# Retention attention into a cosine-gated FFN on one core: a re-planned order, separate scores, and other engines for casts and decay

## The chip, the cores and the metric

The kernel runs on one NeuronCore of a Trainium2 chip. Five engines work from their own instruction queues: TensorE (PE, matrix products; PEld is its weight load), VectorE (DVE), ScalarE (ACT), GpSimd (POOL) and SyncE (SP). DMA transfers are issued from the queues of SP, POOL and ACT and are carried out by 16 DMA engines. The metric is the device time of one execution in microseconds (us). The median of seven runs of the kernel before is 211.03 us (209.88 to 214.27).

## What is computed

Inputs q, k and v are (4 batches, 8 heads, 768 positions, 64), with a decay `lam` per head. Attention is linear with a causal mask and decay, computed over blocks of 64 positions with a carried state:

```python
for b in range(nb):
    intra = np.einsum('bhic,bhjc->bhij', qb, kb) * Dmask[None]
    intra = np.einsum('bhij,bhjd->bhid', intra, vb)
    inter = np.einsum('bhid,bhde->bhie', qb * lam_pow[None], kv_state)
    out[:, :, sl] = intra + inter
    kv_state = lam_block[None, :, None, None] * kv_state + np.einsum('bhsd,bhse->bhde', kb * rev_pow[None], vb)
```

Its output, as 3072 tokens of 512 features, is x of an FFN: `h = x @ w_in` (512 to 2048), `g = h * cos(h)`, `out = g @ w_out` (2048 to 512). All inputs are float32; the kernel multiplies in bfloat16.

## The kernel before

The 3072 tokens are 24 blocks of 128 tokens. Since a decay from position j to i is lam to the power i − j, the kernel multiplies q by one exponential of the position and another operand by the inverse exponential; the mask is then plain 0 and 1 and states need no factor between blocks.

**Opening: two spans.** The first 256 positions of batches 0 and 1 (`SPANS = 2`, blocks 0 to 3) are done by `add_span` in a layout of their own. Six loads (`add_span_load`) of 512 KB each, q0 k0 q1 k1 v0 v1, go out on SP. In `prep` (L547) q is multiplied by `q_sp` and v by `v_sp` into bfloat16, in halves of four heads; who does it stands in `QV` (q by DVE, v by POOL). `prep_k` (L551) casts k on ACT. PE transposes q and k (L558), `transposes_out` (L561) copies them out of PSUM, `scores` (L569) multiplies, `scores_out` (L574) applies the mask on DVE, `values` (L596) and `carried` (L602) make the attention output, `update` (L583) the state for the second half of a span, and `values_out` (L610) casts the output to `xT`, the FFN's input. Meanwhile PE runs idle matmuls (`keep_awake`, L803) in the gaps that the plan foresees.

**Weights.** `add_w` loads w_in in five chunks (`W_IN`, in units of 128 hidden columns: 3, 3, 4, 3, 3) and w_out in four, cast to bfloat16 by the DMA itself, from POOL's queue (L263). The first chunk waits until k1 has landed.

**Pairs.** The remaining 20 blocks are ten pairs, 2 to 11; a pair is the same positions of two batches. `prepare` loads q, k, v (six 256 KB loads on SP, L263), multiplies q and v by the exponentials and casts k, mostly on POOL (L326, L330, L334), and transposes q and k: pair 2 on PE (L356), pairs 3 to 11 by two DMA transposes from SP's queue (L362). `add_scores` makes scores (L404), masks them (L409) and updates the running state (`update` L416, `state` L422), whose bfloat16 copy `S` `state_16` makes on POOL (L427). `add_stretch` makes the values (L465), the part carried by the state (L493) and casts the result to `xT` (L501). Normally the scores and update of the next pair are interleaved in a stretch, between the values of one half and the other; a pair listed in `ALONE` has its scores by themselves, ahead of its own stretch, and the stretch before it begins its second part with a drain of PE.

**FFN.** Blocks are grouped in tiles of four or two (`TILES = [4, 2, 2, 2, 2, 4, 4, 4]`). For each tile and each of 16 groups of 128 hidden columns `hidden` (L683) makes h with four matmuls, `cosine` (L689) runs on ACT, `gated` (L695) on DVE. For the first tile the first `SPLIT` = 4 groups come in two halves, so that the blocks of the first span can start alone. `project` (L726) makes the output of a block, `project_out` (L740) copies it, `store_out` (L747, L749) stores it from SP's queue. PE alternates between hidden products of a tile and output products of the tile before.

**The order.** No queue's order is written by hand. Every instruction is a task with an engine, a duration in us, dependencies and a priority; `Planner.order` runs a list schedule over these estimates and emits the instructions in the order that results. DMAs are two tasks: an issue on a queue and a transfer on one engine called DMA, with a latency `lat` after it. Loads on a queue keep their listed order; transposes and stores are put in among them by the plan. The estimates shape the order alone: on the chip each engine works through its queue in that order and waits for semaphores.

Of the kernel before, what the change touches and what calls it, by code (L numbers as in the profile page):

```python
# [10 lines left out]
F32 = mybir.dt.float32  # L11
# [8 lines left out]
DMA_FROM = 6  # L20
TILES = [4, 2, 2, 2, 2, 4, 4, 4]
SPLIT = 4
BANKS = 8
LAG = 2
ATT = 0.95
ALONE = [3, 4]

QV = [[("DVE", "POOL"), ("DVE", "POOL")], [("DVE", "POOL"), ("DVE", "POOL")]]
OUTS = [{"qT": ("DVE", "DVE"), "kT": ("ACT", "ACT")}, {"qT": ("ACT", "ACT"), "kT": ("ACT", "ACT")}]
V_PRIO = {"POOL": -1.7, "DVE": 0.0}  # L30
LATE = 30.0
ORDER = "q0 k0 q1 k1 v0 v1 i0 i1 i2 i3 i4 o0 o1 o2 o3"

W_IN = [3, 3, 4, 3, 3]

# [15 lines left out]
class Planner:  # L51
# [3 lines left out]

    SETUP = {"POOL": 5.6, "DVE": 5.6, "ACT": 7.3, "SP": 1.3}

# [8 lines left out]
    def order(self):  # L66
# [5 lines left out]
        while todo:  # L72
            first = {}
            for t in todo:
                if only.get(t.eng, t) is not t:
                    continue
                at = self.ready(t, got)
                if at is None:
                    continue
                if t.banks:  # L80
                    b = self.free_banks(t, owner)
                    if len(b) < t.banks:
                        continue
                    t.bank = b[:t.banks]
                    at = max([at] + [x for x, _ in t.bank])
                at = max(at, free.get(t.eng, 0.0))
                first.setdefault(t.eng, []).append((at, t))
            best = None
            for eng, c in first.items():
                t0 = min(a for a, _ in c)  # L90
                a, t = min(((a, t) for a, t in c if a <= t0 + 1e-6), key=lambda x: x[1].prio)
                if best is None or a < best[0]:
                    best = (a, t)
            assert best, "no task can start"
            a, t = best
            t.start, t.end = a, a + t.dur
            free[t.eng] = t.end
            only.pop(t.eng, None)
            if t.then:
                only[t.eng] = t.then  # L100
            if t.get:
                got[t.get].append(t)
            if t.banks:
                t.bank = [i for _, i in t.bank]
                for j, i in enumerate(t.bank):
                    owner[i] = (t, j)
            todo.remove(t)
            done.append(t)
# [30 lines left out]
def kernel(  # L139
# [59 lines left out]
    for i in range(2):  # L199
# [18 lines left out]
                         lnl.unsqueeze(1).to_broadcast([P, NB, H]))  # L218
    v_sp = consts.tile([P, H, 2], F32)
    nc.scalar.activation(v_sp, expo_sp, AF.Exp, scale=-1.0)  # L220
    q_scale = consts.tile([P, NB, H], F32)
# [47 lines left out]
    def add_span_load(name, src, x, prio, deps):  # L269
        def emit(_):  # L270
            if ("raw", x) not in live:
                live["raw", x] = work.tile([P, 3, H, 2, D], F32, tag="g", name="sp_f")
            t = live[name, "sp", x] = live["raw", x][:, "qkv".index(name[0])]
            return start(nc.sync, t.rearrange("u h s d -> u h (s d)"),
                         src[x, :, 0:2 * P, :].rearrange("h (u s) d -> u h (s d)", s=2), deps)

        issue, load_t[name, "sp", x] = dma("SP", 1.5, 0.5, emit, prio, deps)
        return load_t[name, "sp", x]

    def add_load(n, name, src, prio, deps=()):  # L280
# [6 lines left out]

        issue_t[name, n], load_t[name, n] = dma("SP", 1.1, 0.5, emit, prio, deps, get=name)
        return load_t[name, n]
# [3 lines left out]
    def add_w(which, c, prio, deps=()):  # L293
# [7 lines left out]
        part = W_IN[c] / 4 if which == "in" else 1.0  # L301
        _, w_t[which, c] = dma("POOL", 2.6 * part, 0.8, emit, prio - 2000 if which == "in" and c < 2 else prio, deps, lat=2.8 if which == "in" and c < 2 else 1.6)
        return w_t[which, c]
# [8 lines left out]
    def prepare(pr):  # L312
# [51 lines left out]
        for i, src in enumerate((a, k_)):  # L364
            get = None if i else "qkT"
            if 2 * pr >= DMA_FROM:
                head, T[pr, i] = dma("SP", 1.2, 1.3, partial(transposes_dma, i=i), 2 * pr + i - LAG + 1.5,
                                     src + ([qkT_head[pr]] if i else []), get=get, ordered=False)
                T[pr, i].lat = 3.0
                if i and 2 * pr + LAG < NBLK:  # L370
# [20 lines left out]
    def add_scores(pr, part):  # L391
# [34 lines left out]
        def state_16(_, half):  # L426
            nc.gpsimd.tensor_copy(new_S(pr, half), live["sum", pr, half])  # L427

# [17 lines left out]
        if not last:  # L446
            y = pl.add("DVE", 0.69, [x], partial(state, half=1), pa(0.57))
            u.bank_frees.append([y])
            for half, t in enumerate((x, y)):
                if (pr, half) not in Uo:  # L450
                    Uo[pr, half] = pl.add("POOL", 0.61, [t], partial(state_16, half=half), pa(0.56 + 0.02 * half))
        qk_head[pr].frees = [T[pr, 0], T[pr, 1], u]
# [78 lines left out]

    spans, span_deps = [], []

    def add_span(x):
        pa = lambda part: -1000.0 + 2 * x + part
        pv = lambda part: -990.0 + 2 * x + part
        cut = [slice(4 * hp, 4 * hp + 4) for hp in range(2)]
        us = {"DVE": 0.69, "POOL": 1.1}
        vec = {"DVE": nc.vector, "POOL": nc.gpsimd}
        L = {name: consts.tile([P, 2, H, D], BF16, name=f"{name}_sp{x}") for name in ("q", "k", "v")}  # L540
        L.update({name: consts.tile([P, 2, NP, P], BF16, name=f"{name}_sp{x}") for name in ("qT", "kT")})
# [4 lines left out]
        def prep(_, name, hp, e):  # L546
            vec[e].tensor_mul(place(L[name], hp), live[name + "_f", "sp", x][:, cut[hp]],  # L547
                              (q_sp if name == "q" else v_sp)[:, cut[hp]].unsqueeze(3).to_broadcast([P, 4, 2, D]))

        def prep_k(_, hp):  # L550
            nc.scalar.copy(place(L["k"], hp), live["k_f", "sp", x][:, cut[hp]])  # L551

# [59 lines left out]

        so, kt, v_t = [[], []], [], []
        for hp in range(2):
            eq, ev = QV[x][hp]
            a = pl.add(eq, us[eq], [load_t["q_f", "sp", x]], partial(prep, name="q", hp=hp, e=eq), pa(-0.9 + 0.1 * hp))
            kt.append(pl.add("ACT", 0.61, [load_t["k_f", "sp", x]], partial(prep_k, hp=hp), pa(-0.9 + 0.1 * hp)))
            v_t.append(pl.add(ev, us[ev], [load_t["v_f", "sp", x]], partial(prep, name="v", hp=hp, e=ev), pa(V_PRIO[ev] + 0.1 * hp)))
            outs = []
            for name, src in (("qT", a), ("kT", kt[hp])):  # L620
                e = OUTS[x][name][hp]
                t = pl.add("PE", MM(P, 4), [src], partial(transposes, name=name, hp=hp), pa(-0.5 + 0.1 * hp), banks=1)
                outs.append(pl.add(e, 0.58 if e == "ACT" else 0.42, [t], partial(transposes_out, name=name, hp=hp, e=e), pa(-0.5 + 0.1 * hp)))
                t.bank_frees = [[outs[-1]]]
# [3 lines left out]

        u = pl.add("PE", 0.42, v_t + kt, update, -1100.0, banks=1)
        Uo_sp[x] = [pl.add(e, 0.4 if e == "ACT" else 0.42, [u], partial(update_out, h=h, e=e), -1100.0)  # L630
                    for h, e in zip(halves, ("ACT", "DVE"))]
        u.bank_frees = [Uo_sp[x]]
        span_deps.extend(v_t + kt)
        v0 = pl.add("PE", 0.35, so[0] + v_t[:1], partial(values, hp=0), pv(0.2), banks=2)
        v1 = pl.add("PE", 0.35, [v0] + so[1] + v_t[1:], partial(values, hp=1), pv(0.25))
        second = pl.add("PE", MM(P, 4) + 0.1, [v1] + Uo_sp[x], carried, pv(0.3))
        Vo[2 * x] = [pl.add("ACT", 0.6, [v1], partial(values_out, c=0, e="ACT", pairs=slice(0, NP)), pv(0.3))]
        Vo[2 * x + 1] = [pl.add(e, 0.38, [second], partial(values_out, c=1, e=e, pairs=pairs), -1200.0)
                         for e, pairs in (("ACT", slice(0, 2)), ("DVE", slice(2, 4)))]
        v0.bank_frees = [Vo[2 * x], Vo[2 * x + 1]]  # L640
# [26 lines left out]
    def add_ffn(i):  # L667
# [43 lines left out]
        for j in range(nb):  # L711
# [3 lines left out]
            for piece, part in enumerate(pieces):  # L715
# [26 lines left out]
                def store_out(_, eng, j=j, piece=piece, part=part, width=width):  # L742
                    b, c = where(n0 + j)
                    r0 = b * S + c * P
                    if n0 + j < 2 * SPANS:
                        for s, h in enumerate(halves):
# [7 lines left out]
                           get="o_sb")  # L754
                d = dma(queue, 0.7, 1.2 if n0 + j < 2 * SPANS else 0.6, partial(store_out, eng=queue), n0 + j + 8, [e], ordered=False)[1]
                e.frees = [d]
# [8 lines left out]
    for at, name in enumerate(names):  # L765
# [3 lines left out]
        if soft:  # L769
            kept.append(add_w({"i": "in", "o": "out"}[which], n, at, deps))  # L770
        elif n < SPANS and at < 15:
            kept.append(add_span_load(which + "_f", src[which], n, at - 40, deps))
        else:
# [26 lines left out]
    def keep_awake(us, at):  # L800
        cols = P if at < 5.0 else 4 * P
        for _ in range(int(us / (cols / (1200.0 if at < 5.0 else 2400.0) + 0.0025))):
            nc.tensor.matmul(idle_ps[:, :cols], lhsT=ident, rhs=blank[:, :cols], start=True, stop=True)  # L803

    now = 1.6
    for t in plan:
        if t.eng == "PE" and t.start < lead_end.start + 1e-6:
            keep_awake((t.start - now) * 0.95 if now < 2.0 else t.start - now - 0.25, now)
            now = t.end
# [32 lines left out]
```

## Time and profile before

| what | value |
|---|---|
| median of 7 runs | 211.03 us |
| profiled execution, its own time | 210.37 us |
| its span in the profile | 208.7 us |
| PE busy | 193.9 us (93%) |
| DVE, ACT, POOL busy | 111.0, 108.6, 72.2 us |
| first hidden product (L683) | 16.72 us |
| first pair load issued (SP, L263) | 33.76 us |
| last output product ends | 205.25 us |
| granted TensorE clock, mean | 0.998 |
| output products L726 / hidden products L683, busy | 89.1 / 91.2 us |
| HBM read, written | 27.27 MB, 6.29 MB |

Times are from the start of the span. A strip of the page has 40 slices of about 5.2 us, each digit a share of busy time in tenths. Rows of groups give busy time, the mean of one in ns, and the idle time before them with what ended it. In the chain and the timeline a row begins with its start and its length in us; `SPq` and `POOLq` are queues issuing DMAs. "Issue to landing" counts from the issuing instruction's start until the data is there.

### The profile page before, as it was taken

Reading aid. Unit: us, or ns where it says so; the run is one execution under the profiler, and the core shown is the slowest. Engines: PE = TensorE matmul, PEld = TensorE weight load, DVE = VectorE, ACT = ScalarE, POOL = GpSimd, SP = SyncE. Lnnn points to the kernel's source line nnn. Section 1 sums busy time; section 2 is a strip of 40 time slices with the busy share of each in tenths; the row PEclk is TensorE's granted clock in tenths of the full one; section 3 lists DMA queues with packets and bytes.
Section 4 is the critical chain, followed back from the end, with each engine's and each line's share of the span. In section 5 each row is a group of like instructions: output and inputs, shape, how many; then the busy total and the mean of one; then the engine's idle time right before and its main releaser. Section 6 shows DMA issues by size and latency. Waiting matters only on the chain.

```text
span 208.7 us, 5817 instructions
## 1 busy us (share of the span) xinstructions
PE 193.9 (93%) x2426; PEld 112.9 (54%) x2453; DVE 111.0 (53%) x209; ACT 108.6 (52%) x202; POOL 72.2 (35%) x99
## 2 busy tenths in 40 slices
PE   6869999998798999979999999999999999999993
PEld 6447444456656756856765454545444444444462
DVE  2697783263963934966754588746333333333000
ACT  5967771232907644945563676554554555355120
POOL 4099101156156384548483746570000000000000
PEclk9999999999999999999999999999999999999999
DMA  4999999999999999999999999992101110111112
GB/s 126 346 243 141 189 202 219 232 219 224 180 241 170 255 214 265 213 224 246 231 237 249 196 249 202 218 231 81 53 8 42 53 52 0 50 50 53 50 68 82
DMA packets 96234, 34.46 MB, mean 165 GB/s; under 512 B 82256, under 2 KB 93264, under 8 KB 96208
## 3 DMA queue, kind: packets, MB, share of 16 engines
q1 hardware_dynamic: 91312, 29.77, 62.3%
q0 software_dynamic: 4752, 4.19, 13.1%
q8 instruction: 19, 0.31, 0.6%
q10 hardware_dynamic: 144, 0.13, 0.2%
q14 instruction: 7, 0.06, 0.1%
HBM read 27.27 MB, written 6.29 MB: 161 GB/s over the span
## 4 chain that ended last, share of the span: by engine, by line
PE 70%; DMA 15%; SPq 5%; POOL 3%; issue 2%; ACT 2%; DVE 1%; ACTq 0%; POOLq 0%
PE ps_f L726 32%; PE ps_h L683 31%; DMA v_f<-in_v_dram 7%; DMA qkT<-qk 4%; SPq L263 4%; DMA sp_f<-in_k_dram 3%; PE ps_o L465 2%; POOL v_sp L547 1%; PE ps_kv L416 1%; DMA out_dram<-o_sb 1%; PE ps_s L404 1%; ACT cos L689 1%; PE ps_o L493 1%; POOL v_s L334 1%; POOL w_in_sb L263 1%
## 5 line engine op out<-in xcount | busy, mean ns | idle before, releaser
L695 DVE TENSOR_TENSOR g<-ps_h,cos 128x256 bf16<-128x256 f32 (+1 forms) x132 | 70.0, 545 | 54.9 <-ACT cos L689 51.9
L689 ACT ACTIVATE cos<-ps_h,halfpi 128x256 f32<-128x256 f32 (+1 forms) x132 | 71.7, 575 | 41.0 <-PE ps_h L683 40.5
L683 PE MATMUL ps_h<-xT,w_in_sb 128*128 128x256 bf16 (+1 forms) x522 | 91.2, 320 | 0.7 <-ACT o_sb L740 0.4
L726 PE MATMUL ps_f<-w_out_sb,g 128*128 128x512 bf16 (+1 forms) x381 | 89.1, 370 | 1.8 <-issue 1.3
L683 PEld LDWEIGHTS <-w_in_sb 128*128 128x128 bf16 x528 | 51.1, 98 | 34.5 <-issue 0.6
L726 PEld LDWEIGHTS <-g 128*128 128x128 bf16 x400 | 38.3, 98 | 39.0 <-issue 0.3
L326 POOL TENSOR_TENSOR qk<-q_f,q_scale 128x512 bf16<-128x512 f32 x19 | 19.4, 1044 | 33.4 <-DMA q_f<-in_q_dram 26.1
L740 ACT COPY o_sb<-ps_f 128x512 f32<-128x512 f32 (+1 forms) x24 | 13.9, 578 | 24.2 <-PE ps_f L726 21.4
L334 POOL TENSOR_TENSOR v_s<-v_f,v_scale 128x512 bf16<-128x512 f32 x19 | 19.5, 1045 | 6.4 <-DMA v_f<-in_v_dram 6.4
L501 ACT CAST xT<-ps_o 128x512 bf16<-128x512 f32 x19 | 10.2, 588 | 17.8 <-PE ps_o L493 17.0
L409 DVE TENSOR_TENSOR s_m<-ps_s,mask 128x512 bf16<-128x512 f32 x20 | 13.0, 685 | 3.3 <-PE ps_s L404 2.7
L330 POOL CAST qk<-k_f 128x512 bf16<-128x512 f32 x18 | 11.1, 614 | 8.3 <-DMA k_f<-in_k_dram 8.1
L422 DVE TENSOR_TENSOR sum<-sum,ps_kv 128x512 f32<-128x512 f32 x15 | 10.2, 682 | 0.7
L427 POOL CAST S<-sum 128x512 bf16<-128x512 f32 x15 | 9.2, 617 | 1.5 <-DVE sum L422 1.5
L465 PEld LDWEIGHTS <-v_s 64*64 64x64 bf16 x320 | 4.3, 106 | 5.1 <-issue 4.9
L404 PE MATMUL ps_s<-qkT 64*64 64x64 bf16 x320 | 4.4, 194 | 2.8 <-DMA qkT<-qk 1.6
L465 PE MATMUL ps_o<-s_m,v_s 64*64 64x64 bf16 x320 | 6.5, 197 | 0.5
L803 PE MATMUL ps_idle<-blank,ident 128*128 128x128 bf16 (+1 forms) x43 | 5.3, 314 | 1.7 <-POOL ident masks.py:199 1.6
L263 POOL DMA_DIRECT2D w_in_sb<-in_moe_w_in_dram x5 | 4.0, 802 | 6.7 <-DMA sp_f<-in_k_dram 6.7
L740 DVE COPY o_sb<-ps_f 128x256 f32<-128x256 f32 x1 | 0.4, 425 | 10.8 <-PE ps_f L726 10.8
L803 PEld LDWEIGHTS <-ident 128*128 128x128 bf16 x45 | 4.6, 141 | 1.7 <-POOL ident masks.py:199 1.6
L330 ACT CAST qk<-k_f 128x512 bf16<-128x512 f32 x2 | 1.2, 618 | 8.3 <-DMA k_f<-in_k_dram 8.3
(69 smaller groups left out, 81.3 us busy)
## 6 DMA issues: line engine op xcount, KB each, us to landing
q_f<-in_q_dram SPq DMA_DIRECT2D x20, 256.0 KB, 3.5
k_f<-in_k_dram SPq DMA_DIRECT2D x20, 256.0 KB, 4.5
v_f<-in_v_dram SPq DMA_DIRECT2D x20, 256.0 KB, 4.9
out_dram<-o_sb SPq DMA_DIRECT2D x19, 256.0 KB, 2.0
w_out_sb<-in_moe_w_out_dram POOLq DMA_DIRECT2D x4, 512.0 KB, 13.0
w_in_sb<-in_moe_w_in_dram POOLq DMA_DIRECT2D x4, 384.0 KB, 6.6
out_dram<-o_sb SPq DMA_DIRECT2D x9, 128.0 KB, 2.4
sp_f<-in_q_dram SPq DMA_DIRECT2D x2, 512.0 KB, 5.3
```

Of the source, the lines that this page charges most:

```text
L263: i = queue.dma_start(out=o, in_=x)
L326: vec[e].tensor_mul(new_qk()[:, 0, :, s], live.pop(("q_f", 2 * pr + s)), q_scale[:, c, :].unsqueeze(2).to_broadcast([P, H, D]))
L330: (nc.scalar.copy if early else nc.gpsimd.tensor_copy)(new_qk()[:, 1, :, s], live.pop(("k_f", 2 * pr + s)))
L334: vec[e].tensor_mul(live["v_s", 2 * pr + s], live.pop(("v_f", 2 * pr + s)), v_scale[:, c, :].unsqueeze(2).to_broadcast([P, H, D]))
L409: nc.vector.tensor_mul(t, live["s", pr][s], mask.unsqueeze(1).to_broadcast([P, H, D]))
L422: nc.vector.tensor_add(new, live["sum", pr, 0] if half else live["sum", pr - 1, 1], live["kv", pr][half])
L465: yield lambda h=h: nc.tensor.matmul(o[halves[h % 2], h // 2, m], lhsT=live["v_s", n0 + s][m, h, :], rhs=live["s_m", n0 + s][m, h, :], sta ...
L683: nc.tensor.matmul(t[:, :n], lhsT=w_in_sb[:, kd, f * P:(f + 1) * P], rhs=live["xT", i][:, kd, at], start=(kd == 0), stop=(kd == KD - 1))
L689: nc.scalar.activation(c[:, :n], live["h", i, f, at.start][:, :n], AF.Sin, bias=halfpi)
L695: nc.vector.tensor_mul(live["g", i][:, f, at], live.pop(("h", i, f, at.start))[:, :n], live.pop(("c", i, f, at.start))[:, :n])
L726: nc.tensor.matmul(live["f", i, j, piece][:, :width], lhsT=live["g", i][:, f, j * P:(j + 1) * P], rhs=w_out_sb[:, f, part], start=(f == 0) ...
L740: (nc.scalar.copy if eng == "ACT" else nc.vector.tensor_copy)(o[:, :width], live["f", i, j, piece][:, :width])
```

## The change

Four things change together, and with them the plan and so the order of every queue.

1. **Estimates.** Loads are planned with 1.22 us of transfer and 0.85 of issue, stores, DMA transposes, weights and span loads with other durations and latencies; the DMA engine of the plan is free only from 2.9 us, and its tasks are served in the order of their issue. `keep_awake` fills the planned gaps without the margin of 0.25 us.
2. **Structure.** `ALONE` holds pairs 3 to 6 instead of 3 and 4. The tile of pairs 6 and 7 is split into two tiles of one pair. `SPLIT` is 3. w_in comes in four chunks (3, 5, 4, 4).
3. **State casts.** The 15 casts in `state_16` of `add_scores` move from POOL to ACT. (The one of `add_span_state` stays on POOL.)
4. **Spans.** The inverse exponential multiplies k instead of v: in span 0 by DVE, in span 1 by POOL. v of span 0 is cast to bfloat16 by its DMA, which moves to POOL's queue and waits for k0's landing; v of span 1 stays on SP, waits for k1's landing, and is cast by POOL and ACT in halves. The first weight chunk no longer waits for k1; the second is planned after span 1's k multiplies, the fourth after its v casts. All transposed q and k are copied out by ACT. The second span's output casts are split between ACT and DVE, the first span's are on ACT.

```diff
-TILES = [4, 2, 2, 2, 2, 4, 4, 4]
-SPLIT = 4
+TILES = [4, 2, 2, 2, 2, 2, 2, 4, 4]
+SPLIT = 3
-ALONE = [3, 4]
-QV = [[("DVE", "POOL"), ("DVE", "POOL")], [("DVE", "POOL"), ("DVE", "POOL")]]
-OUTS = [{"qT": ("DVE", "DVE"), "kT": ("ACT", "ACT")}, {"qT": ("ACT", "ACT"), "kT": ("ACT", "ACT")}]
+LOAD_US = 1.22
+ALONE = [3, 4, 5, 6]
+QK = [{"q": ("DVE", "DVE"), "k": ("DVE", "DVE")}, {"q": ("DVE", "DVE"), "k": ("POOL", "POOL")}]
+OUTS = [{"qT": ("ACT", "ACT"), "kT": ("ACT", "ACT")}, {"qT": ("ACT", "ACT"), "kT": ("ACT", "ACT")}]
+VALUES_OUT = [[("ACT",), ("ACT",)], [("ACT", "DVE"), ("ACT", "DVE")]]
-ORDER = "q0 k0 q1 k1 v0 v1 i0 i1 i2 i3 i4 o0 o1 o2 o3"
+ORDER = "q0 k0 q1 k1 v0 v1 i0 i1 i2 i3 o0 o1 o2 o3"
-W_IN = [3, 3, 4, 3, 3]
+W_IN = [3, 5, 4, 4]
...
-        issue_t[name, n], load_t[name, n] = dma("SP", 1.1, 0.5, emit, prio, deps, get=name)
+        issue_t[name, n], load_t[name, n] = dma("SP", LOAD_US, 0.85, emit, prio, deps, get=name, lat=1.0)
...
-                head, T[pr, i] = dma("SP", 1.2, 1.3, partial(transposes_dma, i=i), 2 * pr + i - LAG + 1.5,
+                head, T[pr, i] = dma("SP", 1.4, 1.3, partial(transposes_dma, i=i), 2 * pr + i - LAG + 1.5,
-                T[pr, i].lat = 3.0
+                T[pr, i].lat = 1.2
...
         def state_16(_, half):
-            nc.gpsimd.tensor_copy(new_S(pr, half), live["sum", pr, half])
+            nc.scalar.copy(new_S(pr, half), live["sum", pr, half])
...
-        def prep_k(_, hp):
-            nc.scalar.copy(place(L["k"], hp), live["k_f", "sp", x][:, cut[hp]])
+        def cast_v(_, hp):
+            (nc.scalar.copy if hp else nc.gpsimd.tensor_copy)(span_v[x][:, cut[hp]], live["v_f", "sp", x][:, cut[hp]])
...
+            v_t = [[pl.add(("POOL", "ACT")[hp], 0.61, [load_t["v_f", "sp", x]], partial(cast_v, hp=hp), pa(-1.0 + 0.1 * hp))] for hp in range(2)]
+            w_t["in", 3].issue.deps += v_t[0] + v_t[1]
+            late = w_t["in", 1].issue
...
-                d = dma(queue, 0.7, 1.2 if n0 + j < 2 * SPANS else 0.6, partial(store_out, eng=queue), n0 + j + 8, [e], ordered=False)[1]
+                d = dma(queue, 1.2 if n0 + j < 2 * SPANS else 0.9, 1.7 if n0 + j < 2 * SPANS else 0.75, partial(store_out, eng=queue), n0 + j + 8, [e], ordered=False)[1]
...
-            keep_awake((t.start - now) * 0.95 if now < 2.0 else t.start - now - 0.25, now)
+            keep_awake((t.start - now) * 0.95 if now < 2.0 else t.start - now, now)
```

## The prediction

> **What bounds the kernel now.** I read five views, from wide to narrow. The page's first part says who is busy, its strip says whether transfers are:
>
> ```profile
> PE 193.9 (93%) x2426; PEld 112.9 (54%) x2453; DVE 111.0 (53%) x209; ACT 108.6 (52%) x202; POOL 72.2 (35%) x99
> ...
> DMA  4999999999999999999999999992101110111112
> ```
>
> TensorE is idle for 208.7 − 193.9 = 14.8 us. The DMA engines are at nine tenths or more from 5 to about 140 us, so until there the arrival of data can set what TensorE waits for; after it nothing loads. Next the waits of PE:
>
> ```profile
> PE ps_s L404 <- DMA qkT<-qk: 1.6, 2, 1.4
> ...
> PE ps_o L596 <- POOL v_sp L547: 1.3, 2, 0.8
> PE ps_s L404 <- DVE g L695: 1.0, 1, 1.0
> ...
> PE ps_o L493 <- POOL S L427: 0.4, 1, 0.4
> PE ps_h L683 <- ACT o_sb L740: 0.4, 1, 0.4
> ```
>
> The columns are total, times, longest. The first wait is for transposed q and k that come by DMA. The second belongs to the opening, the others to the middle. I placed each with the timeline. Then the chain that ended last, for the opening:
>
> ```profile
> 4.11 5.99 DMA sp_f<-in_k_dram
> 10.09 0.30 issue
> 10.39 1.25 POOL w_in_sb L263 x2
> 11.65 0.50 issue
> 12.15 3.06 POOL v_sp L547 x3
> 15.24 0.42 PE ps_o L596 x16
> ```
>
> The reader sees k of the second span land at 10.10, two weight issues that waited for it on GpSimd, and the four v multiplies behind those. The timeline has the last multiply end at 16.20, and the hidden product run unbroken from 17.87, with one of its 0.435 us groups done before. Its equivalent start is 17.87 − 0.435 = 17.43. Last, SyncE's own waits and the same chain in the middle:
>
> ```profile
> SPq L362 <- POOL S L427: 8.7, 5, 2.4
> SPq L362 <- POOL v_s L334: 8.1, 9, 1.3
> ...
> 48.06 0.59 ACT xT L501
> 48.72 2.51 DMA out_dram<-o_sb
> 51.33 0.59 ACT o_sb L740
> 51.97 2.38 PE ps_h L683 x20
> ...
> 85.99 4.89 DMA qkT<-qk
> 90.93 0.45 PE ps_s L404 x32
> ```
>
> SyncE's queue stands still behind GpSimd's casts; ACT stands still for 2.69 us (48.64 to 51.33) for a store to free an output buffer; and pair 6's scores start 1.35 us after PE was ready.
>
> From 92 us on, PE does FFN blocks and stretches with hardly an idle piece. So three places can change: the opening, the middle (45 to 92 us), and the instructions PE executes.
>
> **The opening.** Removed are four GpSimd v multiplies of 1.04 us (4.05 us in the timeline) and four ACT casts of k (0.617). Added are k multiplies, two on VectorE (0.69) and two on GpSimd (1.04), and casts of v only for the second span (about 0.61 each, one on GpSimd and one on ACT; row L330). The other v is cast by its own DMA from GpSimd's queue, with no compute.
>
> ACT gains two transposed-q copies (0.59 instead of VectorE's 0.42). ACT is free of its table load only at 7.43, and its copies of the first span then end near 9.8, about when scores began before (9.69). VectorE has q and k of the first span, then q of the second: from 5.63 to about 9.9, against masks that began at 10.22. Both are hidden.
>
> Three moves decide. First, **v of span 0** waits on GpSimd for k of span 0 (about 6.9: both k loads average 5.6 us to landing, the later took 5.99), is issued by 7.9, and at the 6.1 us median of v lands near 14.0. Then come 0.42 values, 0.40 carried, 0.6 copy: first hidden product near 15.5, not 16.72. Second, **v of span 1** moves behind a new wait on SyncE for k of span 1: 10.1 + 6.1 = 16.2, cast 0.61, values 0.42, carried 0.40, copy 0.4: 18.1, against a last copy that ends at 18.74. Behind it on SyncE stand only pair loads, due after 30 us. The k path is not later: 10.1, two multiplies to 12.2, transposes 0.40, copy 0.59, scores 0.42, two masks 1.3: 14.9. Third, **the second weight chunk** moves behind the k multiplies on GpSimd: issued at 12.2, landing after 6.6 to 8.0 us (its group's median and longest), 18.8 to 20.2. Hidden groups 0 to 2 of the first blocks (3 x 0.435 = 1.3 us) fit before 18.1, so the start is equivalent to 18.1 − 1.3 = 16.8: **−0.65 us**. But group 3 is wanted at about 19.4, so up to 0.8 us can go back. The idle matmuls lose their 0.25 us margins, and late data then meets a busy PE; at most one 128x512 piece, 0.2 us, which I put in the range.
>
> A rule bears against the move of v. In the row, k of span 1 lands at 10.10 with SyncE's queue alone on the engines; GpSimd issues no load before 10.39. The Trainium skill, page "DMA: Bandwidth & Descriptors", section "Queues, rings and completion order", says each DMA engine goes round-robin between the queues that have work. Then v and the first weights, issued from 7 to 9 us, take turns with k of span 1. By the row k stays at 10.1 and the gain is 0.65. By the rule, k's last 1.5 us of transfer (the landings of the q and k loads are 1.4 to 1.6 us apart) could double, which moves k, and v of span 1 behind it, by up to 1.5 us: a loss of 0.85. No trace here has both queues loading before 10 us.
>
> The supply gains something too: between 15 and 20 us the engines moved 136 GB/s, between 20 and 25 198, because the third weight chunk stood behind the v multiplies until 16.14. Filling that dip is worth (198 − 136) x 5 / 198 = 1.6 us of transfer at most. Pair 2's loads start when the third w_out chunk has landed, at 33.76, so pair 2 can follow an earlier start by up to 1.6 us; if it could not, PE would only wait at 44.5 instead. I take **−0.7 us** for the opening (between −1.6 and +0.9), nearest to my own working of v.
>
> **The middle.** Idle PE that can go: 0.40 (51.97), 1.04 (57.12), 0.40 (63.05), 0.28 (68.53), 1.35 (90.93): 3.47 us.
>
> *Scores apart.* Pairs 5 and 6 no longer have scores inside the stretch of the pair before. Pair 6's are then due when tile 5 starts, several us later than 89.6, and their transposes, landed at 90.9, are in time: −1.35. It costs instructions that stop overlapping: stretches with the next scores inside took 1.46 (111.72 to 113.18), 1.57 (132.01) and 1.21 (100.86), mean 1.41. One without took 1.08 (157.48 to 158.56), and scores with update alone 0.74 (68.53) to 0.90 (44.48). Apart is 1.08 + 0.78 = 1.86, so 0.45 each, **+0.9 us** for two.
>
> *State casts.* Fifteen casts (9.2 us, 0.617 each) leave GpSimd for ACT, at about 0.6 each (ACT's 128x512 casts take 0.588 to 0.618). ACT works 0.52 of the span; 9 us more is hidden under PE. Queued behind each are cosines, and behind those the gates and PE's banks: without slack one would cost 0.6. The 0.40 at 63.05, where the cast sat in GpSimd's queue among q and k, goes. SyncE's transposes, which waited 8.7 us in five pieces on those casts, issue earlier; this hides unless a transpose is late.
>
> *Order with longer transfers.* The planner now charges loads 1.22 us of transfer and 0.85 of issue (1.1 and 0.5 before), stores 1.7 or 0.75 of issue, and transposes from issue start to landing 1.3 + 1.4 + 1.2 = 3.9 (5.5 before; the page's median is 3.8). The three waits at 52, 57 and 68.5 come from what it did not know: six store issues took SyncE from 47.12 to 51.87, so pair 3's transposes went out at 51.98 although GpSimd had k ready at 48.6. If that is reordered, the 1.72 us go; that the order changes there is likely, that nothing else is late in its place is not. I take half, −0.86.
>
> Sum of the removals: −1.35 − 0.40 − 0.86 = **−2.6 us**.
>
> **One more tile of a pair.** Pairs 6 and 7 get their own tiles: 64 hidden matmuls of 512 columns (0.2158, 4 in 0.863) become 128 of 256 (0.1087, 8 in 0.870): +0.1 us. Sixteen cosines of 0.69 become 32 of about 0.39 to 0.47 (+4 to 5 us of ACT, hidden); 32 gates of 0.43 for 16 of 0.69, +2.7 of VectorE, hidden. Without cover neither fits in PE's 0.435 us per hidden group, but there PE alternates with output products. The last two tiles and the end are unchanged.
>
> **Sum.** −0.7 − 2.6 + 0.9 + 0.1 = −2.3 us against the profiled execution's 210.37 (span 208.7 and 1.67 around it): 208.1. The median of the runs stands 0.66 above that execution, so 208.7.
>
> **Rivals.**
> - *All of it works.* −1.6 in the opening and all 3.47: −1.6 − 3.47 + 1.0 = −4.1, 207.0. For it: every wait named has its own remedy. Against: DMA engines at nine tenths leave no room for everything to be early.
> - *The waits only move.* Only pair 6's wait goes: −1.35 + 1.0 = −0.35, 210.7. For it: the DMA engines are full, so an earlier PE meets the same loads. Against: a pair's SyncE cycle is about 10.3 us (56.36 to 66.36 to 76.60 to 87.36), PE's is 2 x 6.9 + 1.4 = 15.2, so supply gains 5 us a pair.
> - *Slower: the transposes' margin.* The plan trusts 3.9 us where landings range from 2.9 to 5.8. Each of the pairs 3 to 8 whose scores are planned at 3.9 and arrive at 4.9 to 5.8 stops PE 1 to 1.9 us. It decides from three such stops up, since 3 x 1 eats the gain of 2.3; five of 1 us give 208.7 + 5 = 213.7. Against: before, only three landings of nine stopped PE, and issues come earlier now.
>
> **How the numbers follow.** Chances: forecast 0.50 (own range 207.4 to 210.0), all works 0.15, only moves 0.20, slower 0.15. About 0.5%, 1.05 us, is what can be told from no change: 209.98 to 212.09. Faster: 0.49 + 0.15 + 0.03 = 0.67; same: 0.01 + 0.15 + 0.02 = 0.18; slower: 0.02 + 0.13 = 0.15. The range runs from 206.4 (below the second case) to 212.3, leaving out most of the slower case and the edges.
>
> **What the profile after would show.** Right: hidden products unbroken from about 17 us without a wait on w_in_sb; v_sp casts before 17; PE not waiting for qkT; no ACT wait for out_dram near 50; S casts in ACT's rows; PE's stretches of pairs 4 and 5 shorter, with own scores after. Wrong: k of span 1 landing after 11, a wait on the second weight chunk near 19, PE waiting for qkT more than 1.6 us in all, or a wait at pair 2 larger than the start gained.

## The result, and the profile after

The changed kernel takes 208.69 us (median of 14 runs, 208.36 to 209.54) against 211.2 (33 runs): ratio 0.9902, 95% interval 0.988 to 0.9924. The forecast was 208.7. The sum was right; in the profile two of its terms were not, and they cancelled.

The profiled execution took 209.54 us, the slowest of the 14, with a span of 207.8. First part of the page after, then the waits of PE (total, times, longest):

```profile
PE 196.6 (95%) x2468; PEld 117.5 (57%) x2498; DVE 114.0 (55%) x222; ACT 119.0 (57%) x231; POOL 63.2 (30%) x83
```

```profile
PE ps_o L608 <- issue: 1.6, 1, 1.6
...
PE ps_kv L595 <- DMA v_sp<-in_v_dram: 0.8, 1, 0.8
PE ps_h L705 <- ACT xT L622: 0.2, 1, 0.2
```

Every wait of the middle that the forecast named is gone: qkT (1.6), the gate (1.0), the state cast (0.4), the stop behind a full output buffer (0.4). In their place there is one wait without a releaser, in the opening. The chain that ended last shows where:

```profile
7.28 5.26 DMA v_sp<-in_v_dram
12.58 0.38 PE ps_kv L595 x12
...
16.70 0.38 PE ps_kv L595 x13
17.13 0.36 PE ps_o L608 x23
17.50 1.59 issue
19.09 0.28 PE ps_o L608 x5
19.39 0.38 ACT xT L622
19.80 0.83 DVE xT L622 x2
20.66 0.38 ACT xT L622
21.08 8.81 PE ps_h L705 x46
```

The hidden product runs on from 21.08 here; before, it ran on from 17.87. So the opening lost time, and the middle gained more than forecast.

To see where time goes I use one measure below. The weight loads of the FFN's matmuls are recorded without gaps (400 for `g`; 528 before and 588 after for `w_in_sb`), so for each moment one can count the columns that FFN products have done. Times 0.2158 us per 512 columns, that is the FFN's work; the moment less that work is the **time not spent on FFN products**. It rises where PE waits, idles or does attention.

| at us | 25 | 50 | 90 | 197 |
|---|---|---|---|---|
| before | 17.02 | 20.97 | 28.71 | 38.82 |
| changed | 19.39 | 23.03 | 28.71 | 37.96 |

Opening: +2.37. From 25 to 90 us: 9.32 instead of 11.69, −2.37. From 90 on: 9.25 instead of 10.11, −0.86 (pair 6's scores waited just after 90 us before). The end differs by the spans' 0.9.

So from profile to profile the gain is 0.83 us (210.37 to 209.54), and by the medians 2.5: the profiled execution before lies 0.8 us below its median, the changed kernel's 0.85 above. The mean granted clock differs as well. It is at least 0.997 in all 14 runs of the changed kernel and 0.998 in the profile before, but at most 0.992 in 59 of the 86 runs of the kernel before that stand beside the experiments.

### The profile page after: what moved, and what is told of

The parts are those of the page before. It is cut to its first block, busy times and chain, and to the rows that moved or that the text cites. A ratio compares the mean times of both kernels' runs of the same rounds, so it can differ in the third digit from the quotient of the medians.

```text
span 207.8 us, 5959 instructions
## 1 busy us (share of the span) xinstructions
PE 196.6 (95%) x2468; PEld 117.5 (57%) x2498; DVE 114.0 (55%) x222; ACT 119.0 (57%) x231; POOL 63.2 (30%) x83
## 4 chain that ended last, share of the span: by engine, by line
PE 89%; DMA 5%; issue 3%; ACT 1%; DVE 0%; SPq 0%; ACTq 0%
PE ps_h L705 40%; PE ps_f L748 39%; DMA v_sp<-in_v_dram 3%; DMA sp_f<-in_k_dram 3%; PE ps_o L475 2%; PE ps_kv L426 2%; PE ps_s L414 2%; PE ps_o L503 1%; PE ps_o L608 1%; PE ps_t L366 0%; DVE xT L622 0%; PE ps_kv L595 0%; PE ps_idle L826 0%; ACT xT L622 0%; PE ps_s L581 0%
## 5 line engine op out<-in xcount | busy, mean ns | idle before, releaser
L717 DVE TENSOR_TENSOR g<-ps_h,cos 128x256 bf16<-128x256 f32 (+1 forms) x147 | 73.0, 505 | 57.5 <-ACT cos L711 56.9
L711 ACT ACTIVATE cos<-ps_h,halfpi 128x256 f32<-128x256 f32 (+1 forms) x147 | 75.4, 540 | 36.3 <-PE ps_h L705 36.1
L705 PEld LDWEIGHTS <-w_in_sb 128*128 128x128 bf16 x588 | 57.0, 98 | 32.3 <-DVE xT L511 0.4
L826 PE MATMUL ps_idle<-blank,ident 128*128 128x512 bf16 (+2 forms) x27 | 9.2, 467 | 1.9 <-POOL ident masks.py:199 1.6
L437 ACT CAST S<-sum 128x512 bf16<-128x512 f32 x15 | 9.1, 619 | 2.4 <-DVE sum L432 2.2
L826 PEld LDWEIGHTS <-ident 128*128 128x128 bf16 x30 | 3.1, 116 | 4.8 <-issue 2.5
L679 POOL CAST S<-sum 128x512 bf16<-128x512 f32 x1 | 0.6, 610 | 14.9 <-DVE sum L676 14.9
L586 DVE TENSOR_TENSOR s_m_sp<-ps_s,mask_sp 128x512 bf16<-128x512 f32 x8 | 5.0, 680 | 0.1
L426 PE MATMUL ps_kv<-v_s,qk 64*64 64x64 bf16 x288 | 4.7, 194 | 0.0
```

The lines of the kernel that those rows point to most:

```text
L705: nc.tensor.matmul(t[:, :n], lhsT=w_in_sb[:, kd, f * P:(f + 1) * P], rhs=live["xT", i][:, kd, at], start=(kd == 0), stop=(kd == KD - 1))
L711: nc.scalar.activation(c[:, :n], live["h", i, f, at.start][:, :n], AF.Sin, bias=halfpi)
L717: nc.vector.tensor_mul(live["g", i][:, f, at], live.pop(("h", i, f, at.start))[:, :n], live.pop(("c", i, f, at.start))[:, :n])
L826: nc.tensor.matmul(idle_ps[:, :n], lhsT=ident, rhs=blank[:, :n], start=True, stop=True)
```

## The experiments

Each group of kernels ran on one chip with its own runs of the kernel before, whose medians differ (211.36, 212.92, 210.77, 212.51 us in the order below), so each kernel is given as a ratio to the runs of before in its own group. The changed kernel itself did not run in these groups; its 0.9902 is from the runs of the result, and a difference of a few tenths of a per cent to it says little. The theories were formed as the runs came in: **A**, the middle gains 3.3 us by itself and the opening loses; **B**, the pairs' arrival sets the pace to 90 us, so the opening's start is free; **C**, an early start and early loads are needed together; **D**, the second weight chunk is what the opening waits for.

### First group: the two halves, the stop, and the separate scores

**mid_only**, the kernel before with the changed middle: the edits below, and the new durations of pair loads, transposes and stores with the new order of service of DMA tasks:

```diff
-TILES = [4, 2, 2, 2, 2, 4, 4, 4]
-ALONE = [3, 4]
+TILES = [4, 2, 2, 2, 2, 2, 2, 4, 4]
+ALONE = [3, 4, 5, 6]
-            nc.gpsimd.tensor_copy(new_S(pr, half), live["sum", pr, half])
+            nc.scalar.copy(new_S(pr, half), live["sum", pr, half])
...
```

> The kernel before with the changed middle alone (tiles, scores apart, state casts on ACT, the plan's new durations for pair loads, transposes and stores); the opening, the weights' chunks and the idle matmuls stay as they were. Theory A (from the two traces: the middle gained some 3.3 us, the opening lost): 207.4 to 208.4, below the changed kernel's 208.69, with the hidden product unbroken from about 17.9 as before. Rival (the forecast's sum: opening -0.7, middle -1.6): 209.5 to 209.9. Rival 2 (the middle was gained because the opening supplies earlier): 210.5 or more.

Measured: 209.68 us, ratio 0.9944 (0.9918 to 0.997). That is 1.2 us of gain by the ratio (0.6 to 1.7), which holds the forecast's middle (−1.6) and is far from theory A's 3.3. Its FFN starts as early as before (17.02 at 25 us), but the early start meets waits again. PE's waits in mid_only:

```profile
PE ps_t L357 <- POOL qk L327: 1.1, 1, 1.1
PE ps_kv L417 <- POOL v_s L335: 1.0, 1, 1.0
```

The first is pair 2's q, the second pair 3's v. So part of what A put down to the middle was paid for by the later start.

**open_only**, the changed kernel with the middle as before (the edits above undone):

> The changed kernel with the middle as before (tiles, ALONE, state casts on POOL, old durations of pair loads, transposes and stores), the opening changed. Theory A: slower than before, 211.7 to 213.5, with the hidden product unbroken only from 20 to 21 us. Rival (the forecast's opening): 210.2 to 210.8, unbroken from about 17.

Measured: 211.1 us, ratio 0.9984 (0.9943 to 1.0025): no difference. Theory A's late start came (hidden products from 20.39; 20.47 at 25 us, 3.4 us later than before), its loss of time did not, and the rival's start at 17 did not either. At 90 us the kernel stands at 28.28, where before stood at 28.71. But the wait at pair 6 lies just behind that mark, and it is longer here than the 1.35 us before:

```profile
93.59 0.45 PE L414 MATMUL ps_s<-qkT 64*64 64x64 bf16 x32 [1.73 <-DMA qkT<-qk]
```

So with a late start the four waits from 52 to 69 us (2.12 of the 3.47 us) were gone without any edit of the middle, and the fifth was not. Nor is this quite the changed kernel's opening. Planned with the old durations, PE does no hidden product ahead of span 1's values and waits for v of span 1:

```profile
PE ps_kv L595 <- POOL v_sp L563: 1.9, 1, 1.9
```

After that the granted clock is 0.50 from 18.0 to 21.4 us, and its mean is at most 0.992 in all 12 runs. The time is that of a worse opening than the changed kernel's. The two halves multiply to 0.9928, and the whole change measured 0.9902; whether the halves add up cannot be told from this.

**rows**, the changed kernel with its first idle matmuls cut finer:

```diff
-            n = min(cols, 4 * P)
+            n = min(cols, P if at < 5.0 else 4 * P)
```

> The changed kernel with the idle matmuls of the first 5 us cut in pieces of 128 columns as before instead of 512: the same PE time, some 66 more PE instructions ahead of the spans' work, nothing else. Theory A (PE's stop of 1.59 us at 17.5, for which the profile shows no releaser, in the middle of the values of span 1, is a late fetch of PE instructions: the fetch of 16 KB began only at 17.0): the place of the fetch moves to an earlier time and the stop shrinks or goes; hidden product unbroken from about 19.5 or earlier, 207.1 to 208.3. Rival (the stop is a wait for data, weights or masks): the stop stays at the same matmul, 208.4 to 209.0.

Measured: 209.08 us, ratio 0.99 (0.9865 to 0.9935). The stop is gone in this profile (hidden product from 20.2), so the first half of the expectation held; the time is that of the changed kernel, so the second did not. The trace says why the stop comes and goes. PE's instructions arrive in blocks of 16 KB on a DMA queue of their own (the page's third part lists 19 such packets before and in the changed kernel, 20 in rows). The first of them within the span began at 16.67 us in the changed kernel's profile, at 13.37 in rows, where 66 more instructions run ahead of the same place, and at 14.58 to 15.37 in the kernels below whose PE queue is the changed kernel's up to there. In these the stop is 0, 0.31 or 0.36 us. Where it occurs it is at the same matmul, the 24th of that run of 30. That matmul starts 2.33 to 2.42 us after the block began in all three profiles with a stop, of 0.31, 0.36 or 1.59 us; 2.2 to 2.6 us after it in the four without; and 4.5 in rows. The timelines of one_tile and split_chunk (start, length, count, and in brackets the idle time before):

```profile
17.23 0.30 PE L608 MATMUL ps_o<-s_m_sp,v_sp 64*64 64x128 bf16 x7 [0.31 <-issue]
```

```profile
17.75 0.30 PE L608 MATMUL ps_o<-s_m_sp,v_sp 64*64 64x128 bf16 x7 [0.36 <-issue]
```

So the stop is a late fetch of instructions. It need not cost its length: pool_casts below has no stop, waits 1.50 us for weights a little later, and stands at the same 19.39 at 25 us as the changed kernel.

**alone2**, `ALONE = [3, 4]` in the changed kernel:

> The changed kernel with the scores of pairs 5 and 6 inside the stretch of the pair before again (ALONE of two). The forecast's step (apart costs 0.9 of instructions and removes a wait of 1.35): the wait for qkT returns at pair 6, 209.0 to 209.6. Rival (the waits went with the new order, the separation costs and brings nothing): no wait for qkT, 207.7 to 208.3.

Measured: 209.29 us, ratio 0.9894 (0.9844 to 0.9944): no difference from the changed kernel's 0.9902. A wait for qkT came back (0.6), but at pair 3 and not at pair 6, and one of 1.2 for the FFN's input xT, behind the stretch that carries pair 5's scores. Apart costs less than forecast: in the changed kernel's timeline scores with the update alone take about 0.73 and a stretch without them 1.02, together 1.75, against 1.21 to 1.56 (mean 1.42) for a stretch with them, so 0.33 each. It brings about as much as it costs, more cannot be told.

### Second group: the start, the supply, the plan's durations, the casts

**late_start**, 1.5 us of idle matmuls more, ahead of the opening's last half group of hidden products:

```diff
+        if t is hid[2 * SPLIT - 1]:
+            keep_awake(1.51, 20.0)
```

> The changed kernel with seven more idle 128x512 matmuls (1.5 us of PE) ahead of the last half group of the opening; every queue's order is otherwise the same. Theory B (from 45 to 90 us the arrival of the pairs sets the pace, so a later start of the FFN is covered by waits that it takes over): 208.3 to 209.3, the time not spent on FFN products larger by 1 to 1.5 at 30 us and by less than 0.5 at 90 us. Rival (each us by which the hidden product starts later counts, as the forecast's step for the opening has it): 209.9 to 210.5.

Measured: 210.35 us, ratio 0.996 (0.9927 to 0.9994): 1.7 us above the changed kernel's 208.69 and above early_loads on the same chip. Theory B falls: from where the changed kernel starts, each further us counts. The time not spent on FFN products was 20.68 at 25 and 29.90 at 90 us.

**early_loads**, pair loads after the second w_out chunk instead of the third:

```diff
-        deps = [kept[-3 if soft else -2]] if at and (names[at - 1][0] in "io") != soft else []
+        deps = [kept[-3]] if at and (names[at - 1][0] in "io") != soft else []
```

> The changed kernel with the pair loads waiting for the second w_out chunk instead of the third, some 2.7 us earlier; the last two w_out chunks then share the DMA engines with pair 2. PE's, ACT's, VectorE's and GpSimd's order is the same. Theory B (the pairs' arrival sets the pace to 90 us): the time not spent on FFN products at 90 us falls by 1 to 2.5, 206.5 to 207.9. Rival (PE's own work sets it, and w_out comes later): 208.7 to 210, with waits of the output product for w_out between 34 and 45 us.

Measured: 208.69 us, ratio 0.9892 (0.9846 to 0.9939). Neither: no gain, and no wait for w_out.

**old_est**, the changed kernel planned with the old durations of pair loads, transposes and stores, and the old order of service of DMA tasks:

```diff
-        issue_t[name, n], load_t[name, n] = dma("SP", LOAD_US, 0.85, emit, prio, deps, get=name, lat=1.0)
+        issue_t[name, n], load_t[name, n] = dma("SP", 1.1, 0.5, emit, prio, deps, get=name)
...
-                T[pr, i].lat = 1.2
+                T[pr, i].lat = 3.0
...
```

> The changed kernel planned with the old durations of pair loads, transposes and stores, and DMA tasks served by priority; no instruction is added or removed. The forecast's step (the order brought 0.86 of the 1.72 us of waits from 51 to 69 us): 209.3 to 210.6, with PE waits at pairs 3 or 4 again. Rival (the pairs' arrival, not their planned durations, sets the pace): 208.4 to 209.1.

Measured: 214.88 us, ratio 1.0161 (1.0082 to 1.0239): 6 us slower than the changed kernel, beyond every expectation. No instruction is added, but the order is another, the opening's too: as in open_only PE waits 1.9 us for v of span 1, and the granted clock is 0.50 from 18.7 to 22.1 us. At 50 us that is made up (23.24, in the changed kernel 23.03). The time not spent on FFN products is 1.4 higher at 90 us, and between 100 and 110 it grows by 5.3 (1.3 in the changed kernel). PE waits there, and the windows after (length, busy times of five engines, granted clock, DMA share, GB/s) show what follows:

```profile
104.49 0.64 PE L414 MATMUL ps_s<-qkT 64*64 64x64 bf16 x32 [2.59 <-DMA qkT<-qk]
```

```profile
100.00:105.00 5.00, 2.41 (x68) 1.57 (x68) 1.12 (x4) 1.84 (x5) 1.88 (x2) 0.90 1.15 158
105.00:108.00 3.00, 2.67 (x84) 1.88 (x74) 2.21 (x4) 1.07 (x2) 1.85 (x2) 0.60 1.08 243
108.00:112.00 4.00, 4.00 (x32) 2.81 (x30) 2.49 (x6) 3.47 (x8) 1.97 (x4) 1.00 0.90 223
```

Pair 7's transposes went out at 98.67, after GpSimd had waited 3.23 us for q, until 95.02; PE was ready for its scores at 101.9. The windows' clocks are means: taken by 1 us it is 0.50 from 104 to 107. From PE's restart at 104.49 to 107.4 half of the clock is missing, by estimate another 1.4 us.

**pool_casts**, the 15 state casts on GpSimd again:

```diff
-            nc.scalar.copy(new_S(pr, half), live["sum", pr, half])
+            nc.gpsimd.tensor_copy(new_S(pr, half), live["sum", pr, half])
```

> The changed kernel with the 15 state casts on GpSimd again. The forecast's step (0.40 at 63 us): 208.9 to 209.4. Theory B (the casts stood ahead of the q and k casts that the transposes wait for, so pairs arrive later): 209.4 to 210.5, SyncE's transposes waiting behind S. Rival (nothing hangs on them): 208.4 to 208.9.

Measured: 208.5 us, ratio 0.9889 (0.984 to 0.9939): no difference. SyncE's transposes waited 5.8 us behind S again, and it cost nothing. Its profile shows something else, at the place where the stop had hidden it:

```profile
21.77 2.55 PE L705 MATMUL ps_h<-xT,w_in_sb 128*128 128x512 bf16 x13 [1.50 <-DMA w_in_sb<-in_moe_w_in_dram]
```

PE waits for the second weight chunk: 1.5 us here, 1.2 in late_start, 1.1 in one_tile, 0.5 in early_loads, 0.2 in alone2.

### Third group: early start with early loads, durations alone, one tile

**mid_early**, mid_only with early_loads' edit:

> mid_only (opening as before, changed middle) with the pair loads waiting for the second w_out chunk instead of the third. Theory C (after the runs so far: the FFN's start counts fully from about 18.5 us on, as late_start shows; an earlier start, as in mid_only, only meets pairs that have not arrived, so both together are needed): PE starts 2.4 us earlier than in the changed kernel and meets pairs 2 and 3 without a wait, 206.5 to 207.6. Rival (all loads before 45 us share full DMA engines, so what pair 2 gains w_out loses): 209.2 to 210.5, with waits of the output product for w_out between 32 and 40 us.

Measured: 209.28 us, ratio 0.9938 (0.9907 to 0.9969), as mid_only. Theory C falls. The q of pair 2 is asked for 2.8 us earlier than in mid_only and arrives at the same time. SyncE's first pair load and GpSimd's first q multiply, mid_only and then mid_early:

```profile
33.92 1.00 SPq L264 DMA_DIRECT2D q_f<-in_q_dram  x2
...
39.29 1.04 POOL L327 TENSOR_TENSOR qk<-q_f,q_scale 128x512 bf16<-128x512 f32 x1 [6.02 <-DMA q_f<-in_q_dram]
```

```profile
31.16 1.00 SPq L264 DMA_DIRECT2D q_f<-in_q_dram  x2
...
39.38 1.04 POOL L327 TENSOR_TENSOR qk<-q_f,q_scale 128x512 bf16<-128x512 f32 x1 [6.01 <-DMA q_f<-in_q_dram]
```

In six kernels looked at this way (before, changed, mid_only, mid_early, early_loads, rows) that multiply starts between 38.30 and 39.38, with loads issued anywhere from 31.1 to 34.4. Everything ahead of it shares DMA engines that are full, and reordering does not make pair 2 come earlier than about 38 us. An FFN that stands at 17.0 at 25 us gets there too soon and waits 1.1 to 1.3 us (mid_only, mid_early); one at 18.1 does not wait there (split_chunk), and from the changed kernel's start on each us counts (late_start). The turning point lies between 17.0 and 18.1.

**est_only**, the kernel before with the new durations alone:

> The kernel before planned with the new durations of pair loads, transposes and stores, and DMA tasks served in order of issue; no instruction is added or removed. If the order alone carries the middle's gain (1.2 us by the medians of mid_only): 209.6 to 210.6. If the longer durations only pay with scores apart and tiles of a pair: 211 or more. The forecast's step for it, -0.86: 210.3.

Measured: 210.68 us, ratio 1.0015 (0.9984 to 1.0046): nothing. Waits moved: qkT no longer stops PE, but xT does (2.4 us in two), and pair 2's q and pair 3's v (0.9 each).

**one_tile**, `TILES` with pairs 6 and 7 together again:

> The changed kernel with pairs 6 and 7 in one tile of four blocks again. The forecast's step (the split costs 0.1 and is otherwise neutral): 208.3 to 208.9. Rival (a tile of four needs pair 7 before its first full-width product, and pair 7 comes late): 209.3 to 211, with PE waiting for qkT between 90 and 110 us.

Measured: 209.65 us, ratio 0.9975 (0.9948 to 1.0002), against 0.9902 of the result: the split is worth about 0.7%, 1 to 1.5 us (the two intervals do not overlap). The time is the rival's, the wait is not: it is xT, not qkT. The chain in one_tile:

```profile
107.91 5.61 PE ps_f L748 x26
...
114.51 0.44 PE ps_o L503 x32
114.95 1.07 ACT xT L511 x2
116.02 0.04 issue
116.06 9.66 PE ps_h L705 x44
```

A tile of four needs the attention of both pairs before its first hidden product. PE runs out of output products of the tile before, stretches pair 7 in, and waits 1.21 us for the two casts to xT. With a tile of its own, pair 6 gives hidden products in time. est_only, whose pairs 6 and 7 also share a tile, has the same wait at the same place (1.21 at 116.5). The kernel before has that tile too and no such wait; it comes with the new order.

### Last: the second chunk

**split_chunk**, the changed kernel with the second chunk cut in two:

```diff
-ORDER = "q0 k0 q1 k1 v0 v1 i0 i1 i2 i3 o0 o1 o2 o3"
-W_IN = [3, 5, 4, 4]
+ORDER = "q0 k0 q1 k1 v0 v1 i0 i1 i2 i3 i4 o0 o1 o2 o3"
+W_IN = [3, 2, 3, 4, 4]
```

> The changed kernel with the second w_in chunk (five groups, 640 KB) cut in two, of two groups (256 KB) and three, issued one after the other at the same place; PE's, ACT's, VectorE's and SyncE's queues are the same. Theory D (the opening is longer than forecast because the second chunk takes 8.4 to 9.5 us to land, not the 6.6 to 8.0 of the smaller chunks before, and PE stops for it near 21 us whenever the fetch of instructions does not stop it first): no PE wait for w_in_sb near 20 us, hidden product unbroken from about 19.5, time not spent on FFN products at 25 us about 18.0 instead of 18.5 to 20.7, 207.7 to 208.4. Rival (pair 2 cannot be on the chip before about 39 us whatever the order of the loads, so PE only waits there): the wait for w_in_sb goes and one of equal length comes at pair 2, 208.4 to 209.0.

Measured: 208.38 us (208.22 to 208.78), ratio 0.9812 (0.9765 to 0.9859) to the runs of before on that chip. The wait for w_in_sb is gone and the hidden product runs on from 19.73:

```profile
19.73 4.49 PE L705 MATMUL ps_h<-xT,w_in_sb 128*128 128x256 bf16 x26 [0.21 <-ACT xT L622]
```

Time not spent on FFN products: 18.09 at 25, 21.84 at 50, 27.42 at 90, 36.66 at 197 us, the lowest of all at the end. Theory D holds for the wait, and no wait of equal length came at pair 2. By the medians the gain is small: the same chip gave 208.5 and 208.69 us for pool_casts and early_loads, and the changed kernel had 208.69 elsewhere. It is the fastest here, by 0.1 to 0.3 us, which the runs do not separate from nothing.

## Why the prediction was right, and where it was not

**The number: partly luck.** The forecast carried the 0.66 us from the profiled execution up to the median over to the changed kernel, whose profiled execution lies 0.85 above its median. From profile to profile it expected −2.3 and got −0.83; the medians, with whatever part the clock has in them, gave −2.5. In the profile the opening cost 2.4 us instead of bringing 0.7, and the rest brought 3.2 instead of 1.6. That the sum came out at 208.7 is luck.

**Opening, −0.7: wrong.** The FFN's start moved back by 1.1 (split_chunk), 1.5 (rows, early_loads) to 2.4 us (changed, pool_casts), and open_only took the time of before (0.9984). Three terms of the working failed.
- *The second weight chunk*: 6.6 to 8.0 us were taken from a group of mostly 384 KB. With 640 KB it took 9.0 us (8.4 in rows), issued at 12.2, and where the stop does not cover it PE waits up to 1.5 us, not 0.8. The prediction named this wait as a sign of being wrong; five profiles show it. split_chunk shows the cause: 256 KB land in 5.8, and the wait is gone.

```profile
w_in_sb<-in_moe_w_in_dram POOLq DMA_DIRECT2D x1, 640.0 KB, 9.0
w_in_sb<-in_moe_w_in_dram POOLq DMA_DIRECT2D x1, 256.0 KB, 5.8
```

- *v of span 1*: 18.1 left out that the plan puts the state update of the span between cast and values, with the two copies of the state one after the other: 0.38 on PE and 0.36 and 0.43 on ACT and VectorE. The landing itself was right (16.0; forecast 16.2). It also left out what is queued ahead of these copies: cosines on ACT and a gate on VectorE for the first blocks' hidden products. The chain of rows, where no stop hides it:

```profile
17.22 0.74 ACT cos L711 x2
17.95 0.26 ACT kv_bd L599
...
18.23 0.43 DVE kv_bd L599
...
18.69 0.42 DVE g L717
19.12 0.67 DVE xT L622 x2
...
19.81 0.38 ACT xT L622
```

- *k's path*, forecast to end at 14.9: the masks ended at 16.45. PE waited 0.75 us for v of span 0, and the second transposes and scores of span 1 were queued behind it. I had not asked what stands behind that wait. v of span 0 came at 12.54, not 14.0. This miss did not set the time: v of span 1 was cast only at 16.65.

No view of before suggested the late fetch, up to 1.6 us.

**The rule on the DMA queues.** By it k of span 1 could have come 1.5 us later. It came as before: in the changed kernel GpSimd's multiply of it starts at 10.22, with v of span 0 issued at 7.28 and weights at 8.35; the landing was 10.10 before. The row was the better guide, and the rule was hardly put to the test: from 7.3 to 9.1 us only SyncE's queue moves data (0.62 MB), and from 9.1 to 9.8 GpSimd's moves its first 0.03 MB beside SyncE's last 0.09. The working took the issue for the start of the transfer; here 1.85 us lie between the two.

**Supply, up to 1.6 us for pair 2: wrong.** Pair 2's q is used from 39.2, after 38.9 before. The dip from 15 to 20 us was filled in part (183 GB/s for 136), but from 30 to 40 the engines moved less than before (171 and 199 for 210 and 226), and the w_out chunk that the pair loads wait for landed at 34.37 instead of 33.74. Asking earlier did not bring them forward either (mid_early).

**The middle, −2.6 of waits and +1.0 of instructions: the size was right, the causes partly not.** All 3.47 us went, and mid_only gained 1.2 (0.6 to 1.7) for the net 1.6. But I treated the waits as independent of the opening. In open_only 2.12 us of them are gone with a later start and no edit of the middle; in mid_only other waits take their place. That is in part why a wrong sign in the opening did little harm: starting late and waiting are then the same time, counted in two places.
- *Scores apart*, −1.35 and +0.9: with the split in place it measured nothing either way (alone2), and pair 6's wait also goes with the new order alone (est_only). The price was 0.33 each, not 0.45; the timeline of before gives as much, 0.99 and 0.74 against a mean of 1.39.
- *State casts*, −0.40: nothing (pool_casts).
- *Order*, −0.86: nothing alone (est_only), and 6 us within the changed kernel (old_est). The term has no value of its own; the plan is made of all durations together.
- *One more tile*, +0.1: here is the sign that I missed. I priced PE's and ACT's instructions and not what a tile of four waits for: xT of its second pair, 1.21 us. No row of before has this wait, since it comes with the new order; the split earns by keeping it away.

**Rivals.** "The waits only move" is the one nearest to the mechanism (full DMA engines, an earlier PE meets the same loads), though not to the time. The transposes' margin did not decide: in the changed kernel no PE wait for qkT is left, in alone2 one of 0.6. In old_est, planned with more time for transposes and less for loads, one of 2.59 came.

**Still open.** How much of the gain by the medians is the clock's: on three chips the runs of before with a mean clock of at most 0.992 have medians 0.1, 1.1 and 1.2 us above those of its other runs, and no run of the changed kernel is among the former. Why old_est is so much worse than before, which has the same durations, is not settled beyond the waits at span 1 and pair 7 and the clock after them. Nor is it known in how many of the changed kernel's 14 runs the fetch stops PE, and for how long.

## What to carry to other kernels

A late start and a wait further on can be the same microsecond: before adding up their removal, find the transfer that both lead to, and ask whether anything makes it land earlier. When a chunk is made larger or a tile wider, price what has to be complete before its first use, not only the instructions. And when an edit adds a wait, list what is queued behind it on that engine; when it adds a step to a path, list what is queued ahead of it.

## What was not expected of the hardware

- PE stopped for 0.3 to 1.6 us in the middle of a run of matmuls, with nothing to wait for, when a 16 KB block of its own instructions began to arrive at 14.9 to 16.7 us, and went on 2.33 to 2.42 us after that; with 66 more instructions ahead, and the block at 13.4, it did not stop.
- After one wait of 2.59 us in old_est PE's granted clock was 0.50 for 3.4 us, so the wait cost about half as much again. The same followed waits of 1.9 us in the openings of open_only and old_est, and did not follow the stop of 1.59 us in the changed kernel or the wait of 1.73 us in open_only.
- GpSimd's first packets moved 1.85 us after its issue began (9.13 after 7.28) in the changed kernel, and 1.80 us after it before (12.19 after 10.39).
- Pair loads issued 2.8 us earlier arrived at the same time (39.29 and 39.38) while the DMA engines were full.
